# Attention followed by two MLPs: engines that take their tasks in listed orders, found anew

## The chip, the cores and the metric

The kernel runs on one core of one Trainium2 chip. The metric is the device time of one execution in microseconds, as the median of several runs; lower is better. The core has five instruction streams that run side by side and meet only at semaphores: TensorE (PE; its weight loads are listed as PEld), VectorE (DVE), ScalarE (ACT), GpSimd (POOL) and the sync engine (SP), which here issues nearly all DMAs. Each stream runs its instructions in the order in which the program emitted them: an instruction that waits holds up all that stand behind it on the same engine.

## The reference

Attention with a halved query sequence, and behind it two MLPs without gating, all in float32 (cut to what matters):

```python
def _attn_ref(q, k, v):                     # (2, 8, 1152, 64) each
    q_pool = q.reshape(B, H, S // 2, 2, D).mean(axis=3)
    scores = scale * np.matmul(q_pool, k.transpose(0, 1, 3, 2))
    scores = scores - np.max(scores, axis=-1, keepdims=True)
    attn = np.exp(scores)
    attn = attn / (np.sum(attn, axis=-1, keepdims=True) + 1e-09)
    return np.matmul(attn, v)

x = attention output as (1152, 512)         # batch and 576 queries by heads
h = x @ w_in;  g = np.maximum(0.01 * h, h);          x = g @ w_out    # 512 -> 2048 -> 512
h = x @ w_in2; g = h * (1.0 / (1.0 + np.exp(-h)));   x = g @ w_out2
```

## The kernel before, in words

**Precision.** Products that need it are made of three matmuls of rounded parts: an operand is split into a high part (ScalarE copies it into the rounded type: `q_high` line 655, `k_high` line 658) and a low part (the rest: `q_low` 661, `k_low` 664, GpSimd or VectorE). Weights are split in the same way (lines 388 and 392) after five conversion steps on ScalarE and VectorE (341 to 360) that start from the buffer `wraw`, into which SP loads a piece (line 317).

**Attention.** The 16 heads are worked in 8 pairs p = 0 to 7; each pair has two halves c of the 576 queries (256 and 320) and nine key tiles t. For a pair: load k, q and v (`load`, `load_v`); pool q on GpSimd (line 652); split; products of the high parts for the maxima (`max_tile`, PE line 734, VectorE maximum 740; the last 64 queries of both heads in `rest_tile`, PE 765, VectorE 769); the maxima become a row (`first_rows` 786 to 805 for pair 0 over TensorE, `finish_max` and DMAs `row<-mn` for the others); `scores` (PE 865) with the row subtracted; exponentials (ScalarE 871) into the tiles `e`; their sum over key tiles in `late` (`sum_first` 896, `sum_up` 909, on VectorE or GpSimd); and the product with v (`pv`, PE 923, three key tiles at a time), taken out by ScalarE (949). `sums` (lines 958 to 1000) then forms the normaliser of a pair: TensorE sums `late` over partitions (963), ScalarE copies it to `sum` (971), and four dependent DMA steps on SP follow: `d<-sum`, `cmp<-d`, VectorE's reciprocal of `cmp` (997), `d<-cmp`, and two `xh<-d` that spread it over partitions. `cmp` has one place. For pairs 4 to 6 the product with the normaliser stands in the MLP part (1043 to 1045); the last pair's own end is lines 1014 to 1036. Before the first maxima, GpSimd also sets constants (`widen`, lines 1095 to 1100).

**MLPs.** The hidden width is worked in four blocks of 512, the tokens in two groups (512 and 640). `layer_in_plain` (1470) makes the first block's input product, `cell` (1516) the others by a scheme of seven products in place of eight, of which the sums are on VectorE (1540) and one copy on ScalarE (1554). `rectify` (1438 to 1448) applies the function on ScalarE and makes the low part on GpSimd; `layer_out_t` (1591) and `layer_out` (1657) form the outputs; `transform` (1377 to 1398) prepares the next layer's operands. SP stores (1684) write the output.

**What sets the order.** Nothing is scheduled on the chip. When the program is built, a planner (`Plan`, `AttentionPlan`; one plan for attention with 1206 tasks, one for the MLPs with 1588) simulates the engines. Each task has an engine, a weight (its assumed length), a due time, predecessors with lags, and tokens that it takes and gives (buffers, PSUM banks). `Plan.run` goes through the engines; one that is idle picks, among its tasks that are ready and whose tokens are free, the one with the smallest `rank`, and emits its instructions. Due times come from the table `DUES`, one number per task, in hundredths of a microsecond:

```python
can = [t for t in ready[e] if t["at"] <= now and all(self.can(x, t["take"].count(x)) for x in t["take"])]
t = min(can, key=lambda t: self.rank(t, now))
```

`rank` is the due time, plus `stay` times the extra cost that a task has at that moment (a change of TensorE's mode, or a port that the planner holds busy for VectorE and GpSimd); `stay`, `stay_mode` and `stay_port` are 0. `whole` gives the lag and weight of the loads of pairs 0 to 2. A tile of the pool is handed out in the order in which it is asked for at emission, and the framework sets the waits for buffers.

Of the kernel before, what the change touches and what calls it, by code (L numbers as in the profile page):

```python
# [7 lines left out]
F32 = mybir.dt.float32  # L8
# [10 lines left out]
def pooled_attention_two_mlps(  # L19
# [61 lines left out]
    stay_mode=0.0,  # L81
    stay_port=0.0,
# [17 lines left out]
    stay=0.0,  # L100
# [12 lines left out]
    name: [int(x) / 100 for x in text.split()] for name, text in dict(attention="""  # L113
# [298 lines left out]
class Plan:  # L412
# [60 lines left out]
    def run(self):  # L473
# [4 lines left out]
        for t in self.tasks:  # L478
            if not t["left"]:
                ready[t["engine"]].append(t)  # L480
# [1299 lines left out]
```

## Time and profile before

| | us |
|---|---|
| median of 3 runs (lowest, highest) | 606.61 (605.55, 607.59) |
| the profiled execution, its own time | 607.19 |
| its span (first to last instruction) | 605.3 |
| TensorE busy in it | 586.3 |
| VectorE, GpSimd, ScalarE busy | 495.3, 358.0, 331.9 |
| attention on TensorE | 1.3 to 211.7 |
| MLPs on TensorE | 211.6 to 602.0 |

The span is shorter than the execution's time by 1.89 us, which lie before the first and after the last instruction. A row of waits names the waiting instruction, then what ended the wait. In a timeline a row is the start in us, the length, the engine, the line, the instruction with its tiles (out<-in) and in brackets the idle time before it with its releaser; several equal instructions in a row are put together (x and their number).

### The profile page before, as it was taken

Reading aid. Unit: us, or ns where it says so; the run is one execution under the profiler, and the core shown is the slowest. Engines: PE = TensorE matmul, PEld = TensorE weight load, DVE = VectorE, ACT = ScalarE, POOL = GpSimd, SP = SyncE. Lnnn points to the kernel's source line nnn. Section 1 sums busy time; section 2 is a strip of 40 time slices with the busy share of each in tenths; the row PEclk is TensorE's granted clock in tenths of the full one; section 3 lists DMA queues with packets and bytes.
Section 4 is the critical chain, followed back from the end, with each engine's and each line's share of the span. In section 5 each row is a group of like instructions: output and inputs, shape, how many; then the busy total and the mean of one; then the engine's idle time right before and its main releaser. Section 6 shows DMA issues by size and latency. Waiting matters only on the chain.

```text
span 605.3 us, 11529 instructions
## 1 busy us (share of the span) xinstructions
PE 586.3 (97%) x4444; PEld 500.5 (83%) x4444; DVE 495.3 (82%) x797; ACT 331.9 (55%) x573; POOL 358.0 (59%) x257
## 2 busy tenths in 40 slices
PE   8899998999999988999999999998999999999997
PEld 6668666686677667999999999898898988988896
DVE  5798788898989978968988978998987798898343
ACT  3748455576475555756545546656765753644231
POOL 7938676476683155877465555787954564546320
PEclk9999999999999999999999999999999999999999
DMA  7222532454143214233333223312332332332102
GB/s 235 79 79 62 157 81 81 108 185 129 19 133 115 76 42 150 82 106 106 104 97 111 74 70 106 103 36 71 104 106 73 103 104 81 96 104 70 42 28 88
DMA packets 34751, 57.44 MB, mean 95 GB/s; under 512 B 13804, under 2 KB 15240, under 8 KB 34696
## 3 DMA queue, kind: packets, MB, share of 16 engines
q1 hardware_dynamic: 34552, 56.50, 30.7%
q8 instruction: 35, 0.57, 0.4%
q10 hardware_dynamic: 144, 0.20, 0.1%
q14 instruction: 20, 0.16, 0.1%
HBM read 50.99 MB, written 3.60 MB: 90 GB/s over the span
## 4 chain that ended last, share of the span: by engine, by line
PE 77%; DVE 10%; DMA 4%; ACT 3%; issue 3%; POOL 2%; SPq 1%; DVEq 0%; ACTq 0%; POOLq 0%
PE psum L1516 24%; PE psum L1657 16%; PE psum L1591 16%; PE psum L865 10%; PE psum L923 6%; DVE late L909 3%; DVE mx L740 3%; PE psum L734 2%; ACT e L871 2%; DMA wraw<-in_moe_w_in_dram 1%; DMA knat<-in_k_dram 1%; PE psum L1470 1%; DVE wt L360 1%; DMA row<-mn 1%; DMA d<-cmp 1%
## 5 line engine op out<-in xcount | busy, mean ns | idle before, releaser
L1591 PE MATMUL psum<-g,wout 128*128 128x320 f32 (+1 forms) x576 | 102.8, 336 | 2.2 <-ACT a L1448 2.2
L740 DVE TENSOR_REDUCE mx<-psum 128x2 f32<-128x768 f32 x96 | 88.1, 952 | 19.5 <-PE psum L734 11.8
L1657 PE MATMUL psum<-wout,g 128*128 128x512 f32 (+1 forms) x444 | 103.2, 385 | 0.4 <-DVE a L1540 0.2
L1591 PEld LDWEIGHTS psum<-g,wout 128*128 128x128 f32 x576 | 92.0, 188 | 9.5 <-ACT a L1448 2.5
L871 ACT ACTIVATE e<-psum 128x512 f32<-128x512 f32 (+1 forms) x144 | 86.0, 657 | 19.3 <-PE psum L865 17.5
L1657 PEld LDWEIGHTS psum<-wout,g 128*128 128x128 f32 x444 | 80.3, 188 | 16.0 <-DVE late L1540 0.7
L909 POOL TENSOR_TENSOR late<-late,e 128x512 f32<-128x512 f32 (+1 forms) x37 | 53.9, 1457 | 34.6 <-DVE late L909 22.5
L923 PE MATMUL psum<-e,vnat 128*64 128x256 f32 (+1 forms) x576 | 73.2, 408 | 0.0
L1540 DVE TENSOR_TENSOR late<-psum,late 128x256 f32<-128x256 f32 (+3 forms) x84 | 54.8, 653 | 21.9 <-PE psum L1516 19.6
L392 POOL TENSOR_TENSOR wout<-wt,wout 128x512 fp32r<-128x512 f32 x32 | 43.0, 1348 | 42.9 <-ACT wout L388 42.7
L923 PEld LDWEIGHTS psum<-e,vnat 128*64 128x64 f32 x576 | 40.0, 137 | 28.8 <-issue 1.5
L1438 POOL TENSOR_TENSOR g<-a,g 128x512 fp32r<-128x512 f32 (+1 forms) x34 | 50.8, 1503 | 20.7 <-ACT a L1448 18.4
L909 DVE TENSOR_TENSOR late<-late,e 128x640 f32<-128x640 f32 (+1 forms) x73 | 61.4, 881 | 0.6
L392 POOL TENSOR_TENSOR w<-wt,w 128x896 fp32r<-128x896 f32 (+1 forms) x18 | 39.2, 2178 | 34.1 <-ACT w L388 31.0
L1438 POOL TENSOR_TENSOR g<-late,g 128x512 fp32r<-128x512 f32 (+1 forms) x28 | 39.9, 1436 | 26.6 <-ACT late L1448 25.1
L1516 PE MATMUL psum<-xh,w 128*128 128x256 f32 (+1 forms) x224 | 50.5, 296 | 1.6 <-ACT late L1554 1.6
L865 PE MATMUL psum<-qh,kh 64*128 64x320 f32 (+1 forms) x288 | 48.1, 329 | 2.3 <-DVE mx L740 1.2
L1516 PE MATMUL psum<-xh,more 128*128 128x256 f32 (+1 forms) x224 | 49.3, 294 | 0.0
L345 DVE TENSOR_SCALAR psum<-psum 128x512 f32<-128x512 f32 x59 | 40.8, 692 | 7.4 <-ACT psum L341 7.4
L392 POOL TENSOR_TENSOR more<-wt,more 128x896 fp32r<-128x896 f32 x14 | 29.8, 2133 | 26.8 <-ACT more L388 20.7
L341 ACT ACTIVATE psum<-wraw 128x512 f32<-128x512 f32 x59 | 36.9, 626 | 15.8 <-DMA wraw<-in_moe_w_out_dram 10.2
L865 PE MATMUL psum<-row,onesr 64*128 64x320 f32 (+1 forms) x288 | 42.9, 292 | 0.9 <-DMA row<-mn 0.9
(127 smaller groups left out, 1365.8 us busy)
## 6 DMA issues: line engine op xcount, KB each, us to landing
wraw<-in_moe_w_in_dram SPq DMA_DIRECT2D x32, 512.0 KB, 4.1
wraw<-in_moe_w_out_dram SPq DMA_DIRECT2D x32, 512.0 KB, 3.3
vnat<-in_v_dram SPq DMA_DIRECT2D x8, 576.0 KB, 5.6
knat<-in_k_dram SPq DMA_DIRECT2D x7, 576.0 KB, 4.5
qnat<-in_q_dram SPq DMA_DIRECT2D x7, 576.0 KB, 6.0
out_dram<-acc SPq DMA_DIRECT2D x8, 256.0 KB, 3.9
xl<-late SPq DMA_DIRECT2D x7, 288.0 KB, 2.8
xh<-d SPq DMA_DIRECT2D x14, 144.0 KB, 3.6
```

The costliest lines, as they stand in the source:

```text
L345: nc.vector.tensor_scalar(out=tf, in0=tf, scalar1=2.0, scalar2=W_TOP, op0=ALU.max, op1=ALU.min)
L392: self.nc.gpsimd.tensor_tensor(out=lo, in0=tf, in1=hi, op=ALU.subtract)
L740: nc.vector.tensor_reduce(out=mx[p][:, u, c], in_=ps[:, :, 0:KC], op=ALU.max, axis=AX.X)
L865: nc.tensor.matmul(out=ps[:, j, 0:n], lhsT=lhsT[own[j], :], rhs=rhs[own[j], cs], start=m == 0, stop=m == len(terms) - 1)
L871: nc.scalar.activation(out=e_t[h, t], in_=ps[:, :, 0:n], func=ACTF.Exp, scale=scale)
L909: e.tensor_tensor(out=a, in0=e_t[h, 0] if t == 1 else a, in1=e_t[h, t], op=ALU.add)
L923: nc.tensor.matmul(out=vps[h][0][own[j], 0, 0:CW[c]], lhsT=vnat[p][:, j, t, :], rhs=e_t[h, t][:, j, :], start=(t == 0), stop=(t == NKT - 1),)
L1438: (nc.vector if fast else nc.gpsimd).tensor_tensor(out=gl, in0=a(), in1=gh, op=ALU.subtract)
L1516: nc.tensor.matmul(out=box[key][:, bank, 0:n], lhsT=w[:, i, :], rhs=y, start=(kk == 0 and q == 0), stop=(kk == 1 and q == 2),)
L1540: nc.vector.tensor_tensor(out=to, in0=p, in1=y, op=ALU.add)
L1591: nc.tensor.matmul(out=box[x][:, c, 0:n], lhsT=wt[:, ms], rhs=y[:, c * n:(c + 1) * n], start=(f == 0 and y is gh and wt is oh), stop=(f == ...
L1657: nc.tensor.matmul(out=box[x][:, c, 0:n], lhsT=y[:, ts], rhs=wt[:, cs], start=(f == 0 and y is gh and wt is oh), stop=(f == FB - 1 and y i ...
```

## The change

`Plan.run` keeps, per engine, a list of all its tasks sorted by due time and then by number, and an engine may begin only the first task of that list; if it is not ready, the engine stays idle. Tasks without an engine ("-", which only hand tokens on) are still chosen as before. The numbers of `DUES` become ranks, counted per engine from 0: TensorE has 318 in attention and 506 in the MLPs, ScalarE 220 and 350, VectorE 243 and 459, GpSimd 102 and 144, SP 150 and 69. The order that they give differs from that of before on every engine. `whole` gives the planner longer lags and weights for the loads of pairs 0 to 2. `cmp` gets the pool's two places instead of one, and the planner gets edges for the places of `sum`, `d`, `cmp` and `d2`. Three `stay` values are no longer 0. The diff, with the table of numbers cut to its first lines:

```diff
@@ -78,8 +78,8 @@
-    stay_mode=0.0,
-    stay_port=0.0,
+    stay_mode=129.57,
+    stay_port=42.33,
...
-    stay=0.0,
+    stay=60.0,
@@ -110,146 +110,91 @@
 DUES = {
-    name: [int(x) / 100 for x in text.split()] for name, text in dict(attention="""
-0 50 300 0 130 110 280 62 0 193 62 124 186 248 53 402 437 566 601 969 1069 691 1152 626 769 524 591 678 869 981 1242
...
+    name: [int(x) for x in text.split()] for name, text in dict(attention="""
+0 12 2 0 9 1 10 0 0 0 1 2 3 4 1 1 2 2 6 6 7 7 8 3 3 4 4 5 5 0 0 10 8 9 7 9 1 3 2 4 4 6 8 10 3 5 11 11 12 12 6 8 9 12 5
...
 """).items()
 }
@@ -475,6 +420,9 @@
         ends, now, left = [], 0.0, len(self.tasks)
+        line = {e: [t["n"] for t in self.tasks if t["engine"] == e] for e in self.ENGINES}
+        for e in self.ENGINES:
+            line[e].sort(key=lambda n: (-self.tasks[n]["due"], -n))
@@ -483,7 +431,11 @@
                 if idle[e] > now:
                     continue
-                can = [t for t in ready[e] if t["at"] <= now and all(self.can(x, t["take"].count(x)) for x in t["take"])]
+                first = line[e][-1] if self.dues and e != "-" and line[e] else None
+                can = [
+                    t for t in ready[e]
+                    if first in (None, t["n"]) and t["at"] <= now and all(self.can(x, t["take"].count(x)) for x in t["take"])
+                ]
@@ -498,6 +450,7 @@
                 ready[e].remove(t)
+                line[e].remove(t["n"])
@@ -636,7 +589,7 @@
     def whole(p, lag):
-        return dict(lag=lag - 1.1, w=1.7) if p < 3 else dict(lag=lag)
+        return dict(lag=lag + 0.9 * (p == 1), w=2.0) if p < 3 else dict(lag=lag)
@@ -955,6 +908,8 @@
+    gone = {}
+
     def sums(p, after, due):
@@ -976,7 +931,7 @@
         def up():
-            box["cmp", p] = sm_p.tile([128, 4 * C // 128], F32, tag="cmp", name="cmp", bufs=1)
+            box["cmp", p] = sm_p.tile([128, 4 * C // 128], F32, tag="cmp", name="cmp")
@@ -991,13 +946,16 @@
-        x = add("ACT", 0.32, due, act, after=[x], give=("duo",))
-        x = dma(due, down, after=[x], lag=P["lag"] - 1.0)
-        x = dma(due, up, after=[x], lag=P["lag"])
+
+        place_of = lambda name, q: [gone[name, q]] if (name, q) in gone else []
+        x = add("ACT", 0.32, due, act, after=[x] + place_of("sum", p - 1), give=("duo",))
+        gone["sum", p] = x = dma(due, down, after=[x], order=place_of("d", p - 2), lag=P["lag"] - 1.0)
+        gone["d", p] = x = dma(due, up, after=[x] + place_of("cmp", p - 2), lag=P["lag"])
         x = add("DVE", 0.13, due, lambda: nc.vector.reciprocal(out=box["cmp", p], in_=box["cmp", p]), after=[x])
-        x = dma(due, down2, after=[x], lag=P["lag"] - 1.0)
+        gone["cmp", p] = x = dma(due, down2, after=[x], order=place_of("d2", p - 2), lag=P["lag"] - 1.0)
         y = dma(due, lambda: up2(0), after=[x], lag=P["lag"] + 2.0)
-        return [y, dma(due, lambda: up2(1), after=[x], order=[y], lag=P["lag"] + 2.0)]
+        gone["d2", p] = z = dma(due, lambda: up2(1), after=[x], order=[y], lag=P["lag"] + 2.0)
+        return [y, z]
```

By the new ranks, the end of SP's list in attention is: `d<-sum` and `xl` of pair 6 (138, 139), `cmp<-d` of pairs 5 and 6 (140, 141), `d<-cmp` of pairs 6 and 5 (142, 143), the first `xh<-d` of pairs 5 and 6 (144, 145), two loads of w_out (146, 147), the second `xh<-d` of pairs 5 and 6 (148, 149). On VectorE the reciprocal of pair 6 is task 240 of 0 to 242, with two adds behind it; on TensorE the sums of pair 6 are task 311 of 0 to 317. At the start GpSimd's list is: zero, rest, a row of ROW, three low parts of k, q's pooling, two low parts of q, then `widen`; ScalarE's has the third piece of pair 0's q and its rest ahead of pair 1's k.

## Rows read from the trace of the kernel before

**Rows 1.** Page part 1: busy us, share of the span, instructions.

```profile
PE 586.3 (97%) x4444; PEld 500.5 (83%) x4444; DVE 495.3 (82%) x797; ACT 331.9 (55%) x573; POOL 358.0 (59%) x257
```

**Rows 2.** Windows: stretch, length, then busy us of each engine, PEclk, DMA, GB/s.

```profile
0.00:30.00 30.00, 25.12 (x220) 18.87 (x222) 19.60 (x30) 16.07 (x33) 25.57 (x37) 1.00 0.48 158
...
90.00:96.00 6.00, 4.46 (x35) 2.20 (x31) 6.00 (x11) 0.71 (x2) 2.88 (x2) 1.00 0.05 5
96.00:143.00 47.00, 46.55 (x500) 34.69 (x500) 41.92 (x56) 30.70 (x54) 31.27 (x23) 1.00 0.49 139
...
210.00:245.00 35.00, 30.37 (x164) 23.97 (x161) 27.67 (x40) 17.99 (x33) 18.46 (x12) 1.00 0.29 90
245.00:405.00 160.00, 160.00 (x1055) 153.56 (x1055) 139.41 (x250) 93.15 (x157) 104.73 (x68) 1.00 0.30 92
405.00:431.00 26.00, 24.00 (x172) 22.90 (x170) 22.80 (x35) 16.16 (x27) 20.84 (x15) 1.00 0.20 61
```

**Rows 3.** TensorE's waits, whole span: waiter <- releaser: us, times, longest.

```profile
PE psum L1470 <- ACT a L1448: 2.1, 1, 2.1
PE psum L734 <- ACT qh L655: 1.9, 3, 0.8
PE psum L1516 <- ACT late L1554: 1.6, 1, 1.6
...
PE psum L765 <- DVE mx L740: 1.2, 1, 1.2
PE psum L865 <- DMA row<-mn: 0.9, 1, 0.9
```

**Rows 4.** Timeline, startup: GpSimd, ScalarE, TensorE, VectorE (start, length, instruction).

```profile
9.49 0.88 POOL L652 TENSOR_TENSOR qnat<-qnat 128x320 f32<-128x320 f32 x1
...
11.10 1.17 ACT L658 ACTIVATE kh<-knat 128x1152 fp32r<-128x1152 f32 x1 [3.48 <-DMA knat<-in_k_dram]
12.17 0.45 ACT L655 ACTIVATE qh<-qnat 128x320 fp32r<-128x320 f32 x1
...
12.68 0.44 PE L734 MATMUL psum<-kh,qh 64*128 64x384 f32 x2 [0.84 <-ACT qh L655]
...
24.48 0.16 DVE L786 TENSOR_REDUCE xh<-mx 128x4 fp32r<-128x12 f32 x1
```

**Rows 5.** Timeline at 88 to 92: VectorE and GpSimd.

```profile
88.59 3.44 DVE L909 TENSOR_TENSOR late<-late,e 128x512 f32<-128x512 f32 x2
89.49 1.85 POOL L652 TENSOR_TENSOR qnat<-qnat 128x576 f32<-128x576 f32 x1
```

**Rows 6.** Timeline, handover: SP's issues, VectorE, ScalarE.

```profile
201.84 0.33 SPq L317 DMA_DIRECT2D wraw<-in_moe_w_out_dram  x1
...
214.93 0.33 SPq L605 DMA_DIRECT2D d<-cmp  x1
218.53 1.09 SPq L605 DMA_DIRECT2D xh<-d  x2
...
206.76 8.01 DVE L909 TENSOR_TENSOR late<-late,e 128x640 f32<-128x640 f32 x10
214.70 0.20 DVE L997 RECIPROCAL cmp<-cmp 128x9 f32<-128x9 f32 x1
218.74 0.76 DVE L1043 TENSOR_TENSOR acc<-xl,xh 128x576 f32<-128x576 f32 x1 [3.84 <-PE psum L1470]
...
219.39 1.15 ACT L341 ACTIVATE psum<-wraw 128x512 f32<-128x512 f32 x2
```

**Rows 7.** Page part 6: DMA issues, count, KB each, median us to landing.

```profile
wraw<-in_moe_w_out_dram SPq DMA_DIRECT2D x32, 512.0 KB, 3.3
```

**Rows 8.** Timeline at 417 to 421: ScalarE.

```profile
416.88 1.28 ACT L1443 ACT_TABLE_LOAD   x1
...
420.60 0.36 ACT L1554 ACTIVATE late<-psum 128x256 f32<-128x256 f32 x1
```

**Rows 9.** VectorE's instructions by line and form: count, busy us, mean ns.

```profile
L909 DVE TENSOR_TENSOR late<-late,e 128x640 f32<-128x640 f32 x48 | 44.9, 935 | 0.6
```

219 rows, old and new, of the table DUES are left out of this document.

## The prediction

> **What bounds the kernel now.** I read the busy table first: TensorE is busy for 586.3 of the span's 605.3 us, 97% [rows 1]. The program's matmuls stay the same, so an order can win only from the 19.0 us in which TensorE does nothing, and it can lose without such a bound. The windows then show where those 19 us lie: 4.9 in the first 30 us, 1.5 in 90 to 96, 0.45 in all of 96 to 143, 4.6 in 210 to 245, 2.0 in 405 to 431, nothing at all in 245 to 405 [rows 2]. The granted clock is 1.00 in every window, so the clock is no part of the sum. Last comes TensorE's table of waits, where every loss has a releaser [rows 3]: ScalarE, for rectified values, for q's high part and for a copy; VectorE, for maxima; one DMA, for the row of maxima. No releaser of a large wait is an engine that is full; each is an instruction that stood behind others in its queue. An order can mend such waits, and move them.
>
> **What the diff decides.** Before, an engine begins whichever ready task has the smallest due time; afterwards only the first of its list. The trace shows each old list with its times, the table of ranks spells out the new one; the steps below compare the two. The three `stay` values act only in a choice among several ready tasks; with one candidate they decide nothing and I cost them at nothing. `whole` and the edges of `place_of` add no instruction; they alter the planner's clock, which may still decide how tasks of different engines interleave, but within one engine the list is final. The second place for `cmp` is what the new SP order needs: it fills pair 6's sums before pair 5's reciprocals have left, which one place would not allow. Instruction count, DMAs and bytes stay.
>
> **Startup, -1.5 us.** TensorE waits 1.9 us in all for `qh` [rows 3], 0.84 of it at 12.68 [rows 4]. The chain before that: GpSimd pools the third piece of q at 9.49, behind the long list of memsets in `widen` and the low parts of k; ScalarE converts at 12.17, behind pair 0's last `kh` piece and pair 1's whole `kh`, which waited 3.48 us for its DMA [rows 4]. The new lists put this pooling ahead of `widen` and this conversion ahead of pair 1's `kh`, after rest and third piece of k. By their durations the conversion ends at about 9.65 instead of 12.62, so the wait at 12.68 has its cause removed. What is late next: `widen` moves after it and the first score rows still need it; v of pair 0 goes behind pair 1's k and q on SP's queue, with slack until the first product with v; and pair 1's q conversion stands ahead of two exponentials of ScalarE, which then start about a microsecond later. VectorE's step for the second half's first rows ran at 24.48 [rows 4]; counting its maxima back to back, the idle between them taken out, it comes at 20.4 to 20.9. The scores that wait for these rows can't use all of this, since the exponentials of the first half are still ahead of them and later by that microsecond: I take the 1.9 of the `qh` waits less some 0.4 that come back. Bounds: nothing, if the exponentials held back cost what the maxima win; 2.5, half of the 4.88 us idle in this window.
>
> **Middle of attention, -1.0 us.** At 92.95 TensorE waits 1.2 us for a maximum [rows 3]; ahead of it VectorE's two adds took 3.44 us beside GpSimd's pooling [rows 5]. In the new list the rest tile of pair 2 stands before those adds, so that wait goes. Later it waits 0.9 us for a row [rows 3], issued on SP behind a weight load that waited for a conversion; the new list sends the load earlier and the rows of the first half ahead of the second's. Together 2.1 us can go. TensorE's 99% in 96 to 143 [rows 2] came from an order that let an engine pass a blocked task; strict lists wait instead, so I keep 1.0 of 2.1. Bounds -2.0 and +2.0; the upper end is the two old waits coming back elsewhere at their size.
>
> **Handover to the MLPs, 0.** This is the costliest stretch, and the one where the change adds a wait. Before, SP issues the last w_out load of this plan at 201.84. The last attention reciprocal runs at 214.70 behind ten adds of 8.01 us; `d<-cmp` follows at 214.93, and its successor on SP only at 218.53, so 3.6 us for the landing [rows 6]. Afterwards SP's list has, in this order, `cmp` of pairs 5 and 6, `d<-cmp` of 6 and of 5, one `xh` row of each, only then the last two w_out loads, and then the second `xh` row of each. So the two loads and pair 5's normaliser queue behind pair 6's reciprocal; behind these wait ScalarE's conversion of the weights and VectorE's product at 218.74. In exchange two adds (0.80 each) come after the reciprocal on VectorE, and pair 6's sums go two products with v earlier on TensorE. With those 1.6 us and the 2.5 us gained before, the reciprocal comes at 214.7 - 4.1 = 210.6; `d<-cmp` of 6 and 5 are issued by 211.1, land by 214.7, two `xh` issues take 1.1 (218.53's two), the loads leave at 215.8 and 216.2 and land 3.3 us later (median of the page) [rows 7], at 219.1 to 219.5. ScalarE converts from these buffers at 219.39 [rows 6]: just in time. Pair 5's second `xh` row leaves at 216.5 and lands at 220.1 by the same 3.6, 1.4 later than the product at 218.74, where TensorE has a wait of 2.1 us anyway [rows 3]. The new ScalarE list also puts the first rectifications ahead of one conversion of weights, which unties that wait of 2.1 us from it. I weigh gain and loss as equal. Bounds: -1.5, most of that wait, and +3.9, worked out below.
>
> **MLP at 420, -1.6 us.** TensorE waits 1.6 us for the copy `late` (line 1554) [rows 3], which ScalarE does at 420.60; a table load of 1.28 at 416.88, and after it a rectifying pair, a conversion and a transform stand in front [rows 8]. The new list has the copy before that pair, right behind the table load, at 416.88 + 1.28 = 418.2. The two tasks it passes are late by one copy (0.36 us), and their reader is GpSimd with slack. Bounds -2.0 (all idle of that window) and -0.5 (a third of it, if another operand of the same product turns out late too).
>
> **Tail +0.2, new stalls +0.7.** The three last tasks of TensorE are the same, but three output stores instead of two fall close to the end (one extra issue, 0.33 like the one at 214.93 [rows 6], partly hidden). For new waits I take 0.7: at the rate of 96 to 143, 0.45 in 47 us [rows 2], the 180 us from 30 to 210 lose 1.7 to small waits, and I let strict lists raise that by some 40%; the lower end is 0, the upper 1.7, a doubling.
>
> **Sum.** -1.5 - 1.0 + 0 - 1.6 + 0.2 + 0.7 = -3.2 us. The profiled execution took 607.19 us, its span 605.3 and 1.9 around it; it lies 0.6 above the median of 606.61. So span 602.1, and from the median 603.4; I predict 603.5.
>
> **Rivals.** (a) **Gains eaten by VectorE, about 606.6.** Its adds on `late` are stretched where GpSimd works too: 48 adds of 640 columns take 0.935 us on average [rows 9], where the ten of the handover took 0.80 each, so 6.4 us are lost. New neighbours on both engines could add half as much again, 3.2 us, where VectorE is 89% busy (96 to 143 [rows 2]); that would cancel the sum. For it: VectorE releases the wait at 93. Against it: in that window alone it is free for 5.1 us. The two adds at 88.59 took 3.44 together beside a pooling of 1.85 [rows 5], so a single collision can cost some 1.8. The Trainium skill, page "SBUF — State Buffer", section "SBUF: two separate sides", has a rule that speaks for this rival: a VectorE instruction with two SBUF inputs and a GpSimd instruction that reads SBUF share a port pair as an exclusive lock, and the later one is blocked for the whole instruction of the other. By that rule every add that starts within a GpSimd instruction would wait for its end; the trace agrees at 88.59, and the mean of the 48 adds says that the old order mostly kept them apart. (b) **Slower by the SP queue at the handover, 609.4.** Place: the two w_out loads and pair 5's normaliser behind pair 6's reciprocal. If VectorE is not ahead of its old times there, that reciprocal is only the two adds sooner, 214.7 - 1.6 = 213.1, 2.5 later than in the forecast. Then the weights land at 221.6 to 222.0, up to 2.6 after 219.39, and pair 5's row at 222.6, 3.9 after 218.74 [rows 6]; I take +3.5. VectorE not ahead also means no gain at startup and in the middle: 606.6 + 3.5 - 1.6 + 0.9 = 609.4. It decides if the reciprocal is later than about 211. (c) **The change doesn't do what it says**, because the lists are nearly the old orders: 606.6. Against: most engines' ranks differ in hundreds of places.
>
> **How the numbers follow.** A difference of 0.3%, 1.8 us, is about what a measurement of this kernel can tell from none. Forecast (with its own range 600.5 to 605): 0.60. Rival (a) and lesser delays at the handover, with (c): 0.19. Rival (b): 0.21. Faster 0.60, same 0.19, slower 0.21. The range reaches from all gains at their bounds (-2.5 - 2 - 1.5 - 2, less the costs: 598.8, of which 599.5 is held to be in reach) to rival (b) at its price, 609.4, so 599.5 to 609.5.
>
> **What would show it.** Right: TensorE's waits for `qh` near 12.7 and 16.3 gone, the wait at 420 below 0.5, line 765's 1.2 gone, and the last `cmp` reciprocal before 211. Wrong: that reciprocal after 213 with ScalarE or VectorE waiting for `wraw` or `xh<-d` near 220 to 224; adds of line 909 with a mean above 0.98; new waits of TensorE between 245 and 405, where there are none; TensorE idle above 19 us.

## The result, and the profile after

The changed kernel takes 614.92 us (median of 4 runs, 614.69 to 616.52) against 606.67 us for the kernel before (the median of now four runs); the ratio is 1.0143, 95% interval 1.0118 to 1.0167. It is slower by 8.3 us. The forecast was 603.5, and the time lies above the whole range, which ended at 609.5.

Line numbers of the changed file are lower: the adds of line 909 are now 862, the maxima 740 are 693, the rest tile 765 is 718 and its maxima 769 are 722, the scores 865 are 818, the reciprocal 997 is 954, the conversion of weights 341 is 286, the rectification 1443 and 1448 is 1401 and 1406, the product 1470 is 1428. The page of the changed kernel, its busy table and the row of granted clocks:

```profile
span 612.9 us, 11507 instructions
...
PE 590.3 (96%) x4444; PEld 502.5 (82%) x4444; DVE 501.8 (82%) x797; ACT 331.1 (54%) x573; POOL 351.9 (57%) x257
...
PEclk9999999999999987999999999999999999999999
```

TensorE's busy time rose from 586.3 [rows 1] to 590.3 with the same matmuls, and the clock row has a dip in its 15th and 16th slice (214.5 to 245.2 us) that the kernel before did not have. VectorE's busy time rose by 6.5 us with the same instructions: the adds on `late` took 10.4 more (below), others less, above all the 16 sums of line 1335 (1377 before) in the MLPs, 14.0 instead of 20.4.

To see where the time went I cut both spans at the first matmul of the MLPs, 211.6 before and 216.8 after. First two windows of the kernel before that cut so (columns as in the rows ahead of the prediction):

```profile
30.00:211.60 181.60, 177.59 (x1872) 128.62 (x1868) 160.61 (x222) 106.89 (x188) 107.83 (x75) 1.00 0.36 102
211.60:245.00 33.40, 28.77 (x150) 23.11 (x149) 26.07 (x37) 17.99 (x33) 18.46 (x12) 1.00 0.30 94
```

and the windows of the changed kernel:

```profile
0.00:30.00 30.00, 26.39 (x247) 20.66 (x247) 22.20 (x33) 17.66 (x35) 25.04 (x37) 1.00 0.53 178
30.00:216.80 186.80, 178.00 (x1843) 127.32 (x1841) 169.19 (x219) 106.29 (x186) 107.39 (x76) 1.00 0.31 89
216.80:245.00 28.20, 21.63 (x103) 16.28 (x102) 15.70 (x24) 10.70 (x21) 7.62 (x6) 0.82 0.38 99
245.00:405.00 160.00, 159.64 (x1030) 151.38 (x1029) 138.38 (x251) 91.54 (x156) 101.93 (x67) 1.00 0.33 100
405.00:431.00 26.00, 26.00 (x194) 25.93 (x193) 23.09 (x39) 16.72 (x28) 20.91 (x14) 1.00 0.20 62
```

Attention ends 5.2 us later. TensorE's idle time in its first 30 us fell from 4.88 [rows 2] to 3.61, but from there to the MLPs it rose from 4.0 to 8.8. That makes 3.5 of the 5.2; in the other 1.7 TensorE is busy for longer with the same matmuls (204.4 instead of 202.7 us up to the MLPs) at a clock of 1.00, and no run shows why. From the begin of the MLPs to 245 the idle time rose from 4.6 to 6.6, and the clock there is 0.82. The idle 2.0 of 405 to 431 [rows 2] is gone. From their first to their last matmul the MLPs took 390.4 us before and take 392.8 now. Idle time hardly changes in sum (+1.9 at the handover, +0.4 from 245 to 405, -2.0 and -0.3 behind), so nearly all of the 2.4 is longer busy time: TensorE works at a lower clock behind the handover.

TensorE's waits, as in [rows 3]:

```profile
PE psum L1428 <- ACT a L1406: 6.0, 1, 6.0
PE psum L718 <- DVE mx L693: 2.8, 2, 1.4
PE psum L818 <- DVE mx L722: 2.2, 2, 2.1
...
PE psum L687 <- ACT qh L608: 0.2, 1, 0.2
```

The waits for `qh`, for line 1512's copy (1554 before) and for the row of maxima are gone or small. In their place stand one wait of 6.0 for a rectified value and 5.0 in all for maxima at the rest tile and the scores, nearly all of it in three waits, at 46.31 (1.41 us), 96.87 (2.05) and 148.39 (1.44).

**VectorE's adds.** Maxima, which read PSUM, and adds on `late`, which read SBUF twice, in VectorE's table of lines; the first row is that of the adds before:

```profile
L909 DVE TENSOR_TENSOR late<-late,e 128x640 f32<-128x640 f32 (+1 forms) x73 | 61.4, 881 | 0.6
...
L693 DVE TENSOR_REDUCE mx<-psum 128x2 f32<-128x768 f32 x96 | 88.5, 951 | 15.5 <-PE psum L687 14.0 <-ACT e L824 0.5 <-ACT late L902 0.3
L862 DVE TENSOR_TENSOR late<-late,e 128x640 f32<-128x640 f32 (+1 forms) x73 | 71.8, 1013 | 2.5 <-POOL late L862 2.1
```

The 96 maxima take what they took before (951 ns; 952 in the page of before). The 73 adds take 71.8 us where they took 61.4. The timeline shows why, and who pays; the rows are, at 40 us and then at 90, VectorE's adds, GpSimd's preparation of the next pair's q and k, and TensorE's wait behind:

```profile
39.87 5.52 DVE L862 TENSOR_TENSOR late<-late,e 128x640 f32<-128x640 f32 x3
...
39.80 1.40 POOL L605 TENSOR_TENSOR qnat<-qnat 128x576 f32<-128x576 f32 x1
41.17 1.59 POOL L617 TENSOR_TENSOR kl<-knat,kh 128x384 fp32r<-128x384 f32 x1
42.72 1.99 POOL L614 TENSOR_TENSOR ql<-qnat,qh 128x576 fp32r<-128x576 f32 x1
...
46.31 0.62 PE L718 MATMUL psum<-kh,rest 128*128 128x384 f32 x2 [1.41 <-DVE mx L693]
...
87.17 9.18 DVE L862 TENSOR_TENSOR late<-late,e 128x512 f32<-128x512 f32 x7
...
88.88 1.48 POOL L605 TENSOR_TENSOR qnat<-qnat 128x576 f32<-128x576 f32 x1 [1.07 <-DMA qnat<-in_q_dram]
90.32 4.41 POOL L617 TENSOR_TENSOR kl<-knat,kh 128x384 fp32r<-128x384 f32 x3
...
96.87 0.39 PE L818 MATMUL psum<-qh,kh 64*128 64x256 f32 x2 [2.05 <-DVE mx L722]
```

Three adds at 39.87 take 5.52 us where three undisturbed ones take 2.4 (the ten of [rows 6] took 0.80 each). They start with GpSimd's pooling and run beside three of its instructions; the maximum behind them is late, and TensorE waits 1.41 us. Seven at 87.17 take 9.18, and TensorE waits 2.05. So the waits for "DVE mx" are not waits for slow maxima but for adds ahead of them in VectorE's queue.

Taken one by one, the adds show more. The three at 39.87 end at 41.88, 43.43 and 45.39, each 0.68 us after a GpSimd instruction has ended (41.20, 42.75, 44.70). In the whole trace 19 of the 73 adds take over 1 us, where it was 10 before. Every one of the 19, and of the 10, began while a GpSimd instruction was running and ended 0.55 us (adds of 512 columns) or 0.68 (640 columns) after that instruction's end. Undisturbed adds take 0.67 and 0.81, so a meeting costs nearly all that is left of the GpSimd instruction.

**Handover.** SP's issues, then VectorE, ScalarE and TensorE of the changed kernel:

```profile
208.59 0.53 SPq L558 DMA_DIRECT2D d<-sum  x1
...
209.79 1.04 SPq L558 DMA_DIRECT2D cmp<-d  x2
217.41 0.80 SPq L558 DMA_DIRECT2D d<-cmp  x2
219.48 1.12 SPq L558 DMA_DIRECT2D xh<-d  x2
220.95 0.81 SPq L262 DMA_DIRECT2D wraw<-in_moe_w_out_dram  x2
221.82 1.60 SPq L558 DMA_DIRECT2D xh<-d  x2
...
217.18 0.21 DVE L954 RECIPROCAL cmp<-cmp 128x9 f32<-128x9 f32 x1
...
229.11 0.76 DVE L1001 TENSOR_TENSOR acc<-xl,xh 128x576 f32<-128x576 f32 x1 [2.02 <-DMA xh<-d]
...
225.74 0.62 ACT L286 ACTIVATE psum<-wraw 128x512 f32<-128x512 f32 x1 [8.38 <-DMA wraw<-in_moe_w_out_dram]
...
228.25 0.62 ACT L286 ACTIVATE psum<-wraw 128x512 f32<-128x512 f32 x1 [1.33 <-DMA wraw<-in_moe_w_out_dram]
228.81 0.58 ACT L1401 ACTIVATE g<-psum 128x512 fp32r<-128x512 f32 x1
229.28 0.59 ACT L1406 ACTIVATE a<-psum 128x512 f32<-128x512 f32 x1
...
223.55 0.39 PE L1428 MATMUL psum<-xh,w 128*128 128x512 f32 x1
229.92 0.79 PE L1428 MATMUL psum<-xh,w 128*128 128x512 f32 x1 [5.98 <-ACT a L1406]
```

Pair 6's reciprocal runs at 217.18, `d<-cmp` follows at once, the `xh` rows at 219.48, and the two w_out loads leave only at 220.95. They are issued among four `xh` rows of 144 KB, and ScalarE gets the first at 225.74 and the second at 228.25. The first rectification (line 1401) stands behind the second conversion, so TensorE, whose banks it frees, does nothing from 223.94 to 229.92. The windows behind it show the clock:

```profile
225.00:230.00 5.00, 0.08 (x1) 0.08 (x1) 1.59 (x3) 2.89 (x6) 0.00 (x0) 0.63 0.42 107
230.00:235.00 5.00, 4.87 (x16) 2.77 (x17) 5.00 (x7) 2.06 (x4) 3.31 (x3) 0.50 0.12 20
235.00:240.00 5.00, 5.00 (x27) 3.59 (x27) 2.32 (x4) 3.09 (x6) 0.46 (x1) 0.84 0.37 115
```

The clock falls while TensorE waits, and behind the wait TensorE works at the lower of its two levels, 1.2 of 2.4 GHz, until about 236.

### The profile page after: what moved, and what is told of

It is laid out like the page before. It is cut to its first block, busy times and chain, and to the rows that moved or that the text cites. A ratio compares the mean times of both kernels' runs of the same rounds, so it can differ in the third digit from the quotient of the medians.

```text
span 612.9 us, 11507 instructions
## 1 busy us (share of the span) xinstructions
PE 590.3 (96%) x4444; PEld 502.5 (82%) x4444; DVE 501.8 (82%) x797; ACT 331.1 (54%) x573; POOL 351.9 (57%) x257
## 4 chain that ended last, share of the span: by engine, by line
PE 76%; DVE 12%; DMA 4%; ACT 3%; issue 3%; POOL 2%; SPq 0%; DVEq 0%; POOLq 0%; ACTq 0%
PE psum L1474 25%; PE psum L1615 16%; PE psum L1549 15%; PE psum L818 9%; PE psum L876 5%; DVE late L862 5%; DVE mx L693 3%; PE psum L687 2%; PE psum L1428 2%; ACT e L824 2%; DMA late<-kept 1%; DMA wraw<-in_moe_w_out_dram 1%; DMA cmp<-d 1%; POOL qnat L605 1%; POOL kl L617 1%
## 5 line engine op out<-in xcount | busy, mean ns | idle before, releaser
L1549 PE MATMUL psum<-g,wout 128*128 128x320 f32 (+1 forms) x576 | 105.1, 336 | 0.0
L824 ACT ACTIVATE e<-psum 128x512 f32<-128x512 f32 (+1 forms) x144 | 87.3, 651 | 24.6 <-PE psum L818 22.4
L862 DVE TENSOR_TENSOR late<-late,e 128x640 f32<-128x640 f32 (+1 forms) x73 | 71.8, 1013 | 2.5 <-POOL late L862 2.1
L337 POOL TENSOR_TENSOR wout<-wt,wout 128x512 fp32r<-128x512 f32 x32 | 41.6, 1306 | 54.0 <-ACT wout L333 51.2
L1396 POOL TENSOR_TENSOR g<-a,g 128x512 fp32r<-128x512 f32 (+1 forms) x34 | 48.4, 1436 | 26.4 <-ACT a L1406 18.6
L818 PE MATMUL psum<-qh,kl 64*128 64x320 f32 (+1 forms) x288 | 42.7, 292 | 0.0
```

What stands on the lines that cost most here:

```text
L337: self.nc.gpsimd.tensor_tensor(out=lo, in0=tf, in1=hi, op=ALU.subtract)
L818: nc.tensor.matmul(out=ps[:, j, 0:n], lhsT=lhsT[own[j], :], rhs=rhs[own[j], cs], start=m == 0, stop=m == len(terms) - 1)
L824: nc.scalar.activation(out=e_t[h, t], in_=ps[:, :, 0:n], func=ACTF.Exp, scale=scale)
L862: e.tensor_tensor(out=a, in0=e_t[h, 0] if t == 1 else a, in1=e_t[h, t], op=ALU.add)
L1396: (nc.vector if fast else nc.gpsimd).tensor_tensor(out=gl, in0=a(), in1=gh, op=ALU.subtract)
L1549: nc.tensor.matmul(out=box[x][:, c, 0:n], lhsT=wt[:, ms], rhs=y[:, c * n:(c + 1) * n], start=(f == 0 and y is gh and wt is oh), stop=(f == ...
```

## The experiments

The lists are data, so the first three runs exchange them whole. Only the numbers of `DUES` change; the rank of a task is then its place in the order that the kernel before had. Each ratio is to the kernel before, run again at the same time: its median was 606.1 us beside the first four runs below and 605.0 beside the last three. So times are compared within these two groups, and across them by ratio.

**Old lists in the new program.** Both tables rewritten:

```diff
-0 12 2 0 9 1 10 0 0 0 1 2 3 4 1 1 2 2 6 6 7 7 8 3 3 4 4 5 5 0 0 10 8 9 7 9 1 3 2 4 4 6 8 10 3 5 11 11 12 12 6 8 9 12 5
+0 1 5 0 3 2 4 0 0 1 1 2 3 4 0 1 2 2 4 10 8 7 12 5 8 3 6 6 9 0 0 10 9 7 4 6 1 3 6 7 7 8 2 4 3 5 9 10 11 12 8 10 9 11 13
...
-1 1 0 0 2 5 7 14 3 2 4 6 12 13 19 5 0 16 17 20 21 22 25 7 2 24 27 28 29 30 33 36 35 13 4 31 34 35 37 38 38 39 41 19 5
+0 0 1 1 4 6 8 11 4 2 5 7 9 11 15 6 1 17 19 21 23 25 25 8 3 20 20 26 28 30 31 34 36 21 4 33 33 35 38 40 42 43 47 19 5
...
```

> The changed program with its listed orders, two places for cmp, whole and stay values, but both lists rewritten to the orders that the kernel before had. Theory (the lost time lies in what the new lists say): 606.7, within 1 us of before, VectorE's adds on late at a mean near 0.88 us, no stall over 3 us, clock 1.00. Rival (listing itself, the second cmp place or whole cost time): over 609.

Measured: 604.33 us, ratio to before 0.9973 (0.9949 to 0.9998). Listing, the second place of `cmp`, `whole` and the `stay` values cost nothing; if they do anything it is 0.3% for the better. The adds take 0.90 us in the mean and no wait of TensorE is over 1.7 us, about as expected; only the clock isn't 1.00 throughout (0.93 in 405 to 431, behind a wait of 1.6). In the trace each engine's instructions stand in the order of the kernel before, so the loss lies in what the new lists say. Its handover, for the next run:

```profile
210.70:245.00 34.30, 31.92 (x172) 26.27 (x171) 29.17 (x43) 20.69 (x38) 21.56 (x14) 1.00 0.33 105
```

**New lists for the MLPs alone** (the first of the two hunks above):

> Attention in the order of before, MLPs in the new lists. Theory: the handover stall comes from attention's SP list, so it is not here; TensorE's wait of 1.6 near 420 goes: 604.8, between 603.5 and 606; no clock below 1.00. Rival (the MLP lists make the 6.0 us wait near 224): 610 or more, with the clock falling near 225.

Measured: 601.17 us, ratio 0.9922 (0.9901 to 0.9943). This is the fastest kernel with the whole computation, ahead of both. Its windows at the handover and at 420:

```profile
211.60:245.00 33.40, 31.90 (x169) 25.75 (x167) 28.78 (x40) 19.81 (x37) 14.72 (x11) 1.00 0.35 104
...
405.00:431.00 26.00, 26.00 (x180) 24.63 (x179) 22.23 (x38) 17.59 (x31) 20.78 (x15) 1.00 0.24 66
```

No idle time is left in 405 to 431, where the kernel before had 2.0. At the handover it is 1.5 us, against 4.6 in the kernel before but 2.4 with the old lists in the new program. So the new MLP order does more than was expected of it: the 2.0 at 420, and something between 0.9 and 3.1 at the handover, since two traces with the same order differ by 2.2 there.

**New lists for attention alone** (the second hunk above):

> Attention in the new lists, MLPs in the order of before. Theory: attention ends on TensorE near 216.8 (5.2 later than before), VectorE's adds at a mean near 1.01 us, and TensorE waits 4 to 8 us near 220 to 230 with the clock at 1.2 GHz behind it: 614 to 617. Rival (MLP lists make the stall): about 611, no clock drop.

Measured: 618.29 us, ratio 1.0211 (1.0187 to 1.0235); the MLPs begin at 218.3, TensorE waits 6.8 us at the handover, and its clock is 0.90 in 210 to 245. That is above the expected 614 to 617, and attention ends 1.5 us later than in the changed kernel; in 90 to 146 the clock is 0.97 here. With the first two runs this is a table of four: the attention lists cost 14.0 us with the old MLP lists (618.29 - 604.33) and 13.8 with the new (614.92 - 601.17), by the ratios 14.4 and 13.4; the MLP lists win 3.2 to 3.4, by the ratios 3.1 and 4.1. Each ratio is known to about 0.25%, 1.5 us, and within that the two parts simply add. The stall at the handover is made by the attention lists, and the new MLP order doesn't make it.

**Loads early.** One edit in SP's list of the changed kernel, written here as the list that the ranks spell (p5, p6: pair 5, pair 6):

```diff
+w_out load
 d<-sum p6
 xl<-late p6
 cmp<-d p5
 cmp<-d p6
+w_out load
 d<-cmp p6
 d<-cmp p5
 xh<-d p5
 xh<-d p6
-w_out load
-w_out load
 xh<-d p5
 xh<-d p6
```

> The changed kernel with one edit in SP's list: the last two w_out loads of attention go from behind pair 6's d<-cmp to ahead of it (one before pair 6's d<-sum, one before its d<-cmp). Theory (the 6.0 us wait at 229.9 is ScalarE's conversions waiting for these loads): that wait falls below 2, the clock stays at 1.00, the time falls by 6 to 8 us, to 607 to 609. Rival (pair 5's normaliser rows, or the late reciprocal, hold the stretch): a wait of 4 or more remains near 226 to 230 for another releaser, time over 612.

Measured: 610.11 us, ratio 1.0077 (1.0055 to 1.0099); in ratio 0.7% or 4.0 us below the changed kernel, somewhat less than expected, as a second wait stood behind the first. The clock from 210 to 245 is 1.00, and TensorE's busy time in the MLPs falls from 385.9 to 382.7 us: the lower clock had cost 3.2. What remains, as TensorE, VectorE and ScalarE show it:

```profile
228.51 0.69 PE L972 MATMUL psum<-late,ones 128*32 128x288 f32 x8 [2.52 <-ACT a L1406]
...
225.92 0.76 DVE L1001 TENSOR_TENSOR acc<-xl,xh 128x576 f32<-128x576 f32 x1 [5.30 <-DMA xh<-d]
...
226.72 0.68 ACT L1002 ACTIVATE xh<-acc 128x576 fp32r<-128x576 f32 x1 [3.08 <-DVE acc L1001]
227.30 0.58 ACT L1401 ACTIVATE g<-psum 128x512 fp32r<-128x512 f32 x1
```

VectorE's product with pair 5's normaliser (line 1001) waits 5.30 us for `xh<-d`; its high part on ScalarE (1002) waits for it, and the next rectification (1401) stands behind that, so TensorE waits 2.52. Both theories had a part of it: the loads, and the normaliser behind them.

**Loads and pair 5's normaliser early.** In addition pair 5's chain goes ahead of pair 6's sums on SP, and its reciprocal nine places up on VectorE:

```diff
+w_out load
+cmp<-d p5
+d<-cmp p5
+xh<-d p5
+xh<-d p5
 d<-sum p6
 xl<-late p6
-cmp<-d p5
 cmp<-d p6
+w_out load
 d<-cmp p6
-d<-cmp p5
-xh<-d p5
 xh<-d p6
-w_out load
-w_out load
-xh<-d p5
 xh<-d p6
```

> The changed kernel with the two w_out loads early (here one before and one behind pair 6's cmp) and, in addition, pair 5's normaliser chain ahead of pair 6's sums on SP, its reciprocal nine places earlier on VectorE. Theory (what was left of the stall, 2.5 us at 228.5, is VectorE's product waiting for pair 5's xh rows, with a conversion, a high part and a rectification queued behind it): that wait is below 0.7 and the time 2 us below that of the kernel with the loads alone, near 608. Rival (the late end of attention holds the handover anyway): no gain over 610.

Measured: 607.36 us, ratio 1.0022 (1.0002 to 1.0042). From the changed kernel's 1.0143 that is 1.2%, 7.3 us, for the handover as a whole: 4.0 for the loads and 3.3 for the normaliser. Its windows:

```profile
30.00:219.10 189.10, 180.42 (x1844) 129.70 (x1841) 169.52 (x219) 106.43 (x187) 107.69 (x76) 0.98 0.33 95
219.10:245.00 25.90, 25.42 (x138) 20.80 (x137) 21.21 (x31) 15.63 (x29) 11.55 (x9) 1.00 0.40 122
```

From the begin of the MLPs to 245 TensorE is idle for 0.5 us, and the MLPs as a whole take 383.3 us, no longer than with the new MLP lists alone (384.4). What the attention lists still cost lies ahead: between 30 and 219.1 TensorE is idle for 8.7 us, where that kernel has 4.4, and busy for 180.4 instead of 177.2, at a clock of 0.98.

**Quiet GpSimd.** GpSimd's preparation of q and k reads 16 columns of each piece. The kernel leaves out the rest: of q it stays unpooled, and of the low parts it is set to zero by a memset, which reads nothing:

```diff
 def pool(p, cs, e):
-        e.tensor_tensor(out=x[:, 0, cs], in0=x[:, 0, cs], in1=x[:, 1, cs], op=ALU.add)
+        n = slice(cs.start, cs.start + (16 if e is nc.gpsimd else cs.stop - cs.start))
+        e.tensor_tensor(out=x[:, 0, n], in0=x[:, 0, n], in1=x[:, 1, n], op=ALU.add)
...
-        e.tensor_tensor(out=KL[p][:, cs], in0=knat[p][:, cs], in1=KH[p][:, cs], op=ALU.subtract)
+        n = slice(cs.start, cs.start + 16)
+        e.memset(KL[p][:, cs].bitcast(F32), 0.0)
+        e.tensor_tensor(out=KL[p][:, n], in0=knat[p][:, n], in1=KH[p][:, n], op=ALU.subtract)
```

and `q_low` like `k_low`. With the new lists:

> The changed kernel, but GpSimd's preparation of q and k (pooling of two rows, low parts) reads almost nothing: 16 columns instead of 320 to 576, the rest of the low parts is written by a memset; so rounded scores and unpooled columns, the same number of tasks and the same lists. Theory (the attention part is 5.2 us longer because VectorE's adds are blocked by these GpSimd instructions): the 73 adds take at most 0.87 us in the mean instead of 1.01, and the MLPs begin on TensorE near 212.5 to 213.5 instead of 216.8; with the handover stall left in, 609 to 612. Rival (strict lists make TensorE wait, whatever the adds take): MLPs still begin after 215.5.

Measured: 604.84 us, ratio 0.9986 (0.9974 to 0.9998). VectorE's adds, the first matmul of the MLPs (the first start in the second row), and the handover (line numbers are five higher from line 606 on):

```profile
L867 DVE TENSOR_TENSOR late<-late,e 128x640 f32<-128x640 f32 (+1 forms) x73 | 56.1, 798 | 2.5 <-POOL late L867 2.1
...
L1433 PE MATMUL psum<-xh,w x96: 304/309/797, 208.3 to 255.5; 128*128 128x320 f32 x64, 128*128 128x512 f32 x32
...
212.57 0.81 SPq L262 DMA_DIRECT2D wraw<-in_moe_w_out_dram  x2
...
208.96 0.21 DVE L959 RECIPROCAL cmp<-cmp 128x9 f32<-128x9 f32 x1
...
221.50 0.80 PE L1433 MATMUL psum<-xh,w 128*128 128x512 f32 x1 [6.05 <-ACT a L1411]
```

With the old lists:

> The same edit of GpSimd's preparation with the old lists of both plans. Theory: here fewer adds met it, so less is won: mean of the adds near 0.83 instead of 0.88, MLPs begin near 210 to 211.5 against 211.6; 603 to 605. The gap to the run with new lists, 5.2 us at the begin of the MLPs, shrinks below 2.5. Rival: the gap stays 4 or more.

Measured: 599.43 us, ratio 0.9896 (0.9871 to 0.9920).

```profile
L867 DVE TENSOR_TENSOR late<-late,e 128x640 f32<-128x640 f32 (+1 forms) x73 | 56.4, 812 | 0.6
...
L1433 PE MATMUL psum<-xh,w x96: 304/309/504, 207.5 to 249.3; 128*128 128x320 f32 x64, 128*128 128x512 f32 x32
```

The adds now take 798 and 812 ns in the mean under either list, and the MLPs begin at 208.3 and 207.5. The gap of 5.2 us has become 0.8, and idle time up to the MLPs is 5.0 with the new lists and 5.6 with the old; TensorE's busy time there is still 1.4 longer with the new lists. Both moved further than I had expected (212.5 to 213.5, and 210 to 211.5), probably since the old lists too had lost some of their time to these meetings and since GpSimd's work itself became shorter; the runs don't separate the two. In time, the edit is worth 1.6% (9.5 us) with the new lists and 0.8% (4.7 us) with the old; the difference, 4.8 us, is what the new lists lose by it, known to about 3 us, as four ratios go into it. The run with new lists tells a second thing. Its reciprocal is at 208.96, 8.2 us earlier than in the changed kernel, and the wait at the handover is 6.05, the same as before.

Put together, of the 13.4 us that the attention lists cost beside the new MLP lists by the ratios, 7.3 are the handover and 4.8 VectorE's adds. 1.3 are not told apart; the parts were taken in different kernels, and the clock's dips (below) move such sums. The profiles split it in another way. The spans of the changed kernel and of the new MLP lists alone differ by 13.6 us (612.9 and 599.3): 5.2 lie ahead of the first matmul of the MLPs and 8.4 behind it (392.8 and 384.4). With a quiet GpSimd the 5.2 is 0.8, and the early loads and normaliser take away all of the 8.4 (383.3); but the attention of that run ends 2.3 us later than the changed kernel's, at the lower clock, which hides a part of the gain in its time.

## Why the prediction was wrong

- **Startup, -1.5: the mechanism was right, the size can't be told.** The conversion of q's third piece ends at 9.47 (forecast 9.65), and TensorE's waits for `qh` fell from 1.9 [rows 3] to 0.2. Idle time of the first 30 us fell by 1.3. But with the old lists in the new program the same window has 2.9 us idle and 4.5 with the old attention lists beside the new MLPs, in the same order of instructions, so a difference of 1.3 in one execution is within what this window does by itself.
- **Middle of attention, -1.0: wrong, +4.8 of idle time.** The step that failed is "the rest tile of pair 2 stands before those adds, so that wait goes". That one wait does go: TensorE passes a rest tile at 91.89 without one. But the tile's maxima stand behind the seven adds, so the scores wait 2.05 at 96.87, and two rest tiles elsewhere wait 1.41 and 1.44. I followed the two old waits through the lists and took their sum as the stake. What decides is which GpSimd instruction runs while VectorE adds, for all 73 adds, and the lists tell that only if both are laid on one clock. This is **rival (a)**, which I had priced at +3.2 us of VectorE's time, enough to cancel the gains; it measured +10.4 (71.8 - 61.4), and the sign I gave for it, a mean above 0.98, was met with 1.01. The price of one meeting was too high, and the number of them too low: the two adds of [rows 5] met two GpSimd instructions, not one, and took 0.8 and 1.2 longer than undisturbed ones, but the long adds went from 10 to 19. Its counter-argument, that VectorE is free for 5.1 of 47 us, doesn't hold: an add that is late by a whole GpSimd instruction delays the maximum behind it at once, however much room there is later. The Trainium skill, page "SBUF — State Buffer", section "SBUF: two separate sides", states that the later one of the two waits for the whole instruction of the other; the 19 long adds agree, and the maxima, which read PSUM and kept their 951 ns, are in line with its limit to VectorE instructions with two SBUF inputs. Two adds of the kernel before don't fit: at 167.12 and 191.21 they began within long GpSimd instructions of line 392 and took 0.82 and 0.83, and no run shows why.
- **Handover, 0: wrong; rival (b) was the mechanism, and its price was too low.** The change made exactly the wait that the step named, two loads and pair 5's normaliser behind pair 6's reciprocal. Priced at 3.5, it cost 4.2 against the kernel before (1.9 of idle time and 2.3 of clock) and 8.4 against the new MLP order without it. Four terms were off. The reciprocal came at 217.18, not 210.6, because attention was late where I had it early. The landing of the loads took 4.8 and 6.9 us (220.95 and about 221.4 to the conversions at 225.74 and 228.25), not the page's median of 3.3; four `xh` rows went with them, and whether these were the reason no run tests. I let a conversion that is late cost its own delay, and had the first rectifications ahead of one of them; in the trace both conversions stand ahead of the first rectification (228.81), as before, and through the banks TensorE queues behind it. And the threshold "it decides if the reciprocal is later than about 211" was wrong in kind: I compared new times with the old conversion's 219.39, but the MLPs start when attention ends. With GpSimd quiet the reciprocal is at 208.96 and the stall is still 6.05. The loads leave 4.2 and 4.3 us after the MLPs' first matmul in these two runs, so a gain ahead of the handover doesn't shorten the stall.
- **The clock was in no case.** I noted 1.00 in all windows and left it out. The clock fell during the stall of 6 us, and TensorE's busy time in the MLPs rose by 2.3 us against the kernel before, 3.2 against the run with the loads early, where the clock stayed at 1.00 there.
- **MLP at 420, -1.6: right**, 2.0 us measured. What I missed is the new MLP order's gain at the handover, 0.9 to 3.1, which the attention lists hid.
- **Tail, +0.2:** nothing to see: 3.2 us from TensorE's last matmul before, 3.3 after. **New stalls, +0.7:** in the MLPs 0.4, from 245 to 405; those of attention are in the 4.8 above.
- **The cases.** I made (a) and (b) alternatives, with 609.4 as the worst. Both came, with the clock on top: 609.4 held no loss in attention, and it misses by 5.5 us, about the 5.2 by which attention ends later. Of the gains, only that at 420 shows beyond doubt.
- **Rival (c)** is excluded: with the old lists the new program runs as the kernel before.

## What to carry to other kernels

When orders are fixed per engine, the cost lies between the lists: lay VectorE's two-input SBUF work and GpSimd's work on one time line and count the meetings, and for each queue of loads ask what the loads now stand behind. A wait that hangs on the end of a stage moves with that end, so compare it with the next stage's start and not with an old clock time. Exchange the parts of a change before throwing it away: here one half wins 0.8% on the kernel before (601.17 us), and the other half loses four times as much as that half's lists win.

## What the runs showed of the hardware

- VectorE's adds of 640 columns from SBUF took 0.81 us undisturbed and up to 2.03 us where they began while a GpSimd instruction ran; each of the long ones ended 0.68 us after that instruction, as if it had waited for all of it. Beside GpSimd's memsets, which read nothing, two adds of the quiet kernel took 0.81 and 0.83 (at 108.64 and 111.75) though 0.29 and 0.49 us of the memset were left. The maxima from PSUM kept 0.95 us in the mean in every run.
- The granted clock fell with TensorE's own waits: during 6.0 us of idle time, and it was 0.50 until about 236 us. Around waits of 1.4 and 2.1 us in the middle of attention it stayed at 1.00 in the profile of the changed kernel but shows 0.97 as the mean of 90 to 146 in three of the other runs with these attention lists; so such short waits sometimes come with a dip too, and what decides it the runs don't show. Of the ten runs with loads and normaliser early, the three with a mean clock of 1.00 took 605.2 to 605.4 us, the seven with 0.993 to 0.997 took 606.1 to 607.8.
- Two w_out loads of 512 KB each took 4.8 and 6.9 us to land beside four rows of 144 KB, where the page of the same run has 3.4 as the median of that load.
